# Output tiles in pairs: two-bank accumulators, one VectorE add and one store per pair, a fixed order, and all main stores on one queue

## The chip, the cores and the metric

The kernel runs on one core of one Trainium2 chip. The metric is the device time of one execution in microseconds. All runs quoted here are in the same (fast) state. Before the change the median is 433.73 us (433.66 to 433.82, four runs). A profile is a separate execution and its span is a little shorter than the timed one: 431.5 us for the kernel before.

## The reference

The first part is linear attention. The second part works on its result `x` (8 batches, 576 rows, 512 columns): a Fourier transform along the rows, a complex 512x512 weight for each of the lowest 64 modes, the inverse transform, and a channel product.

```python
def phi(v): return np.where(v > 0, v, np.exp(v) - 1.0) + 1.0
x = (phi(q) @ (phi(k).T @ v)) / (phi(q) @ phi(k).sum(rows) + 1e-6)      # per batch and head (shortened)
X = np.fft.rfft(x, axis=1)
Yr = np.einsum('bmd,mde->bme', Xr, w_r) - np.einsum('bmd,mde->bme', Xi, w_i)   # 64 modes
Yi = np.einsum('bmd,mde->bme', Xr, w_i) + np.einsum('bmd,mde->bme', Xi, w_r)
y = np.fft.irfft(Y, n=S, axis=1)
u = x + y
return u + np.maximum(u @ w_ch, 0.0)
```

## The kernel before

The two weights hold 134 MB in float32 and stream in through GpSimd's queue, with a cast on the way. For each mode four small matmuls per weight give the product. Almost everything else is worked off while the weights stream: `E` = x @ w_ch per output tile, the inverse transform of the modes that are done, and so on. When the last weight has landed, the last modes go into a small tile `last`, copies of its rows go by DMA into the tiles `YZ` of the batches, and the output stage begins.

The output stage has 36 tiles of 128x512: 32 main tiles, and four tail tiles made of the last 64 rows of two batches each. Per tile there is an identity matmul that adds `E` (L526), an inverse transform for the channel half (L507), a relu in place in the tile's accumulator in PSUM (ScalarE, L537; such an accumulator of 128x512 in float32 is called a bank here), a second inverse transform (L507), VectorE's add of `x` (L543), and a store (L548; a tail has two stores of half the partitions, L555). Main tiles are stored in twos, except the first two and the last two.

```python
def keep_warm(n):                                  # dummy matmuls; L333
    for _ in range(n):
        nc.tensor.matmul(last_ps[0], id16, wch16[:, 0, :])

def acc_bank(t):                                   # one bank per tile, from the pools of the weight stage
    ...
    return psW.tile([128, D], F32, tag=tag, bufs=bufs, name=f"acc{t}")

def begin(t, acc=None):
    if acc is None:
        acc = acc_bank(t)
        add_channels(acc, t)                       # E, identity matmul
        add_inverse(acc, t, 1)
    else:
        add_inverse(acc, t, 1, LATE)
    nc.scalar.activation(out=acc, in_=acc, func=AF.Relu)
    return acc

def end(t, acc, single):
    add_inverse(acc, t, 0)
    x = x_of(t)
    nc.vector.tensor_tensor(out=x, in0=acc, in1=x, op=ALU.add)
    ...                                            # main tiles: one store for two tiles unless single
        queue().dma_start(out=..., in_=x_main[b][:, j0 : jj + 1, :])
    ...                                            # tail tiles: two stores of 64 partitions
        (nc.sync, nc.gpsimd)[hf].dma_start(out=..., in_=x_tail[i][hf * 64 : hf * 64 + 64, :])

def queue():                                       # alternates
    return (nc.sync, nc.gpsimd)[n_queue % 2]

# in the mode loop, after mode NM - 5:
    last_ps += [bank("zl0"), bank("zl1")]          # buffers of the rotating tag "bank"
# in the last four modes keep_warm(6) is called after the first weight and after the product
```

A scheduler places the instructions of each engine by their dependencies. `pin` (short for `tc.keep_in_program_order`) fixes an instruction behind the pinned one traced before it on the same engine. The keep-warm matmuls and the output stage before the change are not pinned.

Of the kernel before, what the change touches and what calls it, by code (L numbers as in the profile page):

```python
# [10 lines left out]
F32 = mybir.dt.float32  # L11
F16 = mybir.dt.float16
BF16 = mybir.dt.bfloat16
AF = mybir.ActivationFunctionType
ALU = mybir.AluOpType
# [32 lines left out]
def kernel(  # L48
# [10 lines left out]
    nc = tc.nc  # L59

    B, H, S, Dh = q.shape
    D = H * Dh
# [3 lines left out]
    NJJ = 4  # L66
# [309 lines left out]
    psW = tc.alloc_tile_pool(name="psW", bufs=1, space=bass.MemoryType.PSUM)  # L376
# [23 lines left out]
    for kk in range(n_early):  # L400
# [6 lines left out]
        sW.tile([128, D], F32, tag="x_tail", bufs=B // 2, name=f"x_tail{i}") for i in range(B // 2)  # L407
# [4 lines left out]
    def x_of(t: int):  # L412
        return x_main[t // NJJ][:, t % NJJ, :] if t < B * NJJ else x_tail[t - B * NJJ]
# [10 lines left out]
    def bank(name: str, shape=(128, D), dtype=F32):  # L424
        return psW.tile(list(shape), dtype, tag="bank", bufs=5, name=name)
# [67 lines left out]
    n_acc = 0  # L493

    def acc_bank(t: int):
        nonlocal n_acc
        n = n_acc
        n_acc += 1
        tag, bufs = ("bank", 5) if n < N_PRE or (n - N_PRE) % 8 > 2 else (("P", 2), ("P", 2), ("yt", 1))[(n - N_PRE) % 8]
        return psW.tile([128, D], F32, tag=tag, bufs=bufs, name=f"acc{t}")  # L500

    N_PRE = 3
    EARLY, LATE, BOTH = 1, 2, 3

    def add_inverse(acc, t: int, half: int, what: int = BOTH):

        mm = lambda o, l, r: nc.tensor.matmul(  # L507
            o, l, r, start=False, stop=True, skip_group_check=True
        )
        if t < B * NJJ:  # L510
            parts = [(t // NJJ, slice(0, 128), slice(t % NJJ * 128, t % NJJ * 128 + 128))]
        else:
            i = t - B * NJJ
            parts = [(2 * i + h, slice(h * 64, h * 64 + 64), slice(512, 576)) for h in range(2)]
        for b, r, sel in parts:
            if b > 0:
                mm(acc[r, :], inv_sb[:, sel], YZ[b][:, half, :])
                continue
            if what & EARLY:
                mm(acc[r, :], inv_sb[: 2 * NE, sel], YZ[b][: 2 * NE, half, :])  # L520
            if what & LATE:
                mm(acc[r, :], inv0_sb[:, sel], last[:, half, :])

    def add_channels(acc, t: int):
        for cols, src in e0_parts(t):
            nc.tensor.matmul(  # L526
                acc[:, cols], id16, src, start=(cols.start == 0), stop=False, skip_group_check=True
            )

    def begin(t: int, acc=None):  # L530
        if acc is None:
            acc = acc_bank(t)
            add_channels(acc, t)
            add_inverse(acc, t, 1)
        else:
            add_inverse(acc, t, 1, LATE)
        nc.scalar.activation(out=acc, in_=acc, func=AF.Relu)  # L537
        return acc

    def end(t: int, acc, single: bool):  # L540
        add_inverse(acc, t, 0)
        x = x_of(t)
        nc.vector.tensor_tensor(out=x, in0=acc, in1=x, op=ALU.add)  # L543
        if t < B * NJJ:
            b, jj = divmod(t, NJJ)
            if jj % 2 == 1 or single:
                j0 = jj if single else jj - 1
                queue().dma_start(  # L548
                    out=out[b, 0:512, :].rearrange("(r j) d -> r j d", j=NJJ)[:, j0 : jj + 1, :],
                    in_=x_main[b][:, j0 : jj + 1, :],  # L550
                )
        else:
            i = t - B * NJJ
            for hf in range(2):
                (nc.sync, nc.gpsimd)[hf].dma_start(  # L555
                    out=out[2 * i + hf, 512:S, :], in_=x_tail[i][hf * 64 : hf * 64 + 64, :]
                )

    n_queue = 0

    def queue():
        nonlocal n_queue
        n_queue += 1
        return (nc.sync, nc.gpsimd)[n_queue % 2]

    order = []
    for i in range(B // 2):
        order += [2 * i * NJJ + jj for jj in range(2 * NJJ)]
        order.insert(len(order) - 2, B * NJJ + i)
    single = set(order[:2] + order[-2:])  # L570
    ready = {}
# [4 lines left out]
    for kk in range(n_early, NM):  # L576
# [9 lines left out]
        if kk == NM - 5:  # L586
            for t in order[:N_PRE]:
                acc = ready[t] = acc_bank(t)
                add_channels(acc, t)
                add_inverse(acc, t, 1, EARLY)  # L590
            last_ps += [bank("zl0"), bank("zl1")]


    y_ps = psW.tile([128, NDC, 128], F16, tag="P", bufs=2, name="ypl")
# [18 lines left out]
    for b in range(1, B):  # L613
        eng = nc.sync if b < 3 else nc.gpsimd
        eng.dma_start(out=YZ[b][2 * NE : 128, :, :], in_=last[b::B, :, :])  # L615


    SKEW = 2
    accs = {}
    for n in range(len(order) + SKEW):  # L620
        if n < len(order):
            accs[n] = begin(order[n], ready.get(order[n]))
        if n >= SKEW:
            t = order[n - SKEW]
            end(t, accs.pop(n - SKEW), t in single)
    psW.release()
# [29 lines left out]
```

## Time and profile before

| | before |
|---|---|
| time, median | 433.73 us |
| DMA share until 390 us | about 1.06 (full) |
| last weight landed | 394.0 us |
| first add of the output stage | 399.01 us |
| end of the last add | 424.6 us |
| span of the profile | 431.5 us |

The table by windows of the kernel before. Its columns are named in its first line; PEclk is the TensorE clock granted, 1.00 being full, and DMA share is how busy the 16 DMA engines were. In all views PE is TensorE and PEld its weight loads, DVE is VectorE, ACT ScalarE, POOL GpSimd and SP SyncE; L507 is line 507 of the kernel; a line of dots marks a cut.

```profile
core 0: us, PE busy (x) PEld busy (x) DVE busy (x) ACT busy (x) POOL busy (x), PEclk, DMA share, GB/s
340.00:344.00 4.00, 2.46 (x18) 1.06 (x15) 1.64 (x4) 0.72 (x2) 1.06 (x2) 0.50 1.06 213
...
384.00:388.00 4.00, 3.27 (x23) 1.34 (x23) 0.00 (x0) 0.58 (x1) 0.00 (x0) 1.00 1.07 214
...
396.00:400.00 4.00, 4.00 (x26) 2.02 (x24) 1.41 (x3) 3.01 (x6) 2.17 (x5) 1.00 0.14 40
400.00:404.00 4.00, 4.00 (x21) 1.45 (x20) 3.08 (x6) 2.82 (x5) 1.36 (x3) 1.00 0.64 238
404.00:408.00 4.00, 4.00 (x22) 1.77 (x19) 4.00 (x7) 3.37 (x6) 1.16 (x2) 1.00 0.86 311
408.00:412.00 4.00, 4.00 (x20) 1.61 (x19) 3.66 (x6) 3.15 (x7) 1.09 (x2) 1.00 0.97 386
...
428.00:432.00 4.00, 0.00 (x0) 0.00 (x0) 0.00 (x0) 0.00 (x0) 0.00 (x0) 0.50 0.06 21
```

At 340 us and at 384 us the DMA engines are full (share 1.06 and 1.07): the weights bound the kernel there, and the matmuls have time to spare (TensorE is busy for 2.46 and 3.27 us of the 4). Note the clock: 0.50 at 340 us, 1.00 at 384 us. From 396 us the output stage runs; TensorE is busy for the whole of each window, and the DMA engines fill up with stores (311 GB/s, then 386).

The dummy matmuls are one group in the view by lines; its last part says when they ran.

```profile
L333 PE MATMUL zl_3714<-wch_67,id_64 x42: 376/379/390, 378.4 to 393.1; 128*128 128x512 f16 x42
```

They stand between 378 and 393 us, in the gaps in which TensorE waits for weights, and the clock is full there (1.00 in every window from 376 to 394 us).

The chain of waits of the kernel before, from the last weight towards the output stage (start, length, what ran; `zl` is the last modes' channel product):

```profile
394.05 0.39 PE P_0_3815 L348 x4
...
395.65 0.61 PE zl_3714 L601 x4
396.26 0.44 PE zl_3715 L601 x4
```

The timeline of VectorE, of ScalarE, and of TensorE in the kernel before (start, length, engine, line, operation):

```profile
399.01 0.69 DVE L543 TENSOR_TENSOR x_main_1602<-acc_3705,x_main_1602 128x512 f32<-128x512 f32 x1 [1.86 <-PE acc_3705 L507]
399.62 0.68 DVE L543 TENSOR_TENSOR x_main_1602<-acc_3708,x_main_1602 128x512 f32<-128x512 f32 x1
...
397.71 0.58 ACT L537 ACTIVATE acc_3705<-acc_3705 128x512 f32<-128x512 f32 x1 [0.18 <-PE acc_3705 L507]
398.21 0.58 ACT L537 ACTIVATE acc_3708<-acc_3708 128x512 f32<-128x512 f32 x1
...
405.18 0.38 PE L507 MATMUL acc_3942<-YZ_1616,inv_sb 128*128 128x512 f16 x1
405.40 0.38 PE L507 MATMUL acc_3929<-YZ_1616,inv_sb 128*128 128x512 f16 x1
```

Back-to-back adds start 0.61 us apart and back-to-back relus 0.50. A matmul of 512 columns starts every 0.215 us at full clock, so the three of a main tile take 0.645 us: TensorE sets the pace of production, by a little. In the view of TensorE's waits there is no entry for the kernel before between 398 and 424 us; around a tail a few matmuls start 0.31 to 0.34 us apart instead of 0.215. The stores need 9.44 MB at up to 400 GB/s (401 from 415 to 416 us), 23.6 us by that rate: nearly as long as the 25.6 us from the first add to the end of the last.

### The profile page before, as it was taken

How to read it: one execution, taken by the hardware profiler on the slowest of the kernel's cores; microseconds unless marked ns; L12 is line 12 of the kernel's file. 1: busy time of each engine (PE TensorE's matmuls, PEld its weight loads, DVE VectorE, ACT ScalarE, POOL GpSimd, SP SyncE). 2: the span in 40 equal slices, each digit the busy share in tenths (PEclk: the TensorE clock that was granted, in tenths of full speed). 3: DMA queues.
4: the chain of work that ended last, by engine and by line, in shares of the span. 5: the costliest groups of instructions: out<-in, count | busy, mean ns of one | idle time of the engine just before them, and what ended most of it. 6: DMA issues, size and time to landing. Idle time of an engine off the chain costs nothing. (4 is left out here: it accounts for less than half of the span.)

```text
span 431.5 us, 6261 instructions
## 1 busy us (share of the span) xinstructions
PE 296.4 (69%) x2544; PEld 153.4 (36%) x2544; DVE 178.7 (41%) x350; ACT 148.8 (34%) x228; POOL 97.8 (23%) x176
## 2 busy tenths in 40 slices
PE   0359677796028677667776767657588759987992
PEld 0347556573004233222322223223233227833340
DVE  1699998954004232322322223223223212202893
ACT  3687666621003222222223222122222221302781
POOL 4232322122112212211222112112112120201321
PEclk9999766666559766685658577586855566999998
DMA  9999999999999999999999999999999999993796
GB/s 151 208 208 209 209 209 209 212 213 218 218 212 213 214 214 213 213 214 214 213 213 213 214 215 213 214 213 213 213 213 213 214 214 213 213 213 70 283 347 263
DMA packets 35468, 92.36 MB, mean 214 GB/s; under 512 B 3200, under 2 KB 16384, under 8 KB 35440
## 3 DMA queue, kind: packets, MB, share of 16 engines
q0 software_dynamic: 33184, 86.69, 100.5%
q1 hardware_dynamic: 2256, 5.28, 3.6%
q8 instruction: 20, 0.33, 0.3%
q14 instruction: 8, 0.07, 0.0%
HBM read 164.07 MB, written 9.44 MB: 402 GB/s over the span
## 5 line engine op out<-in xcount | busy, mean ns | idle before, releaser
L348 PEld LDWEIGHTS <-xt_c 128*32 128x32 bf16 x520 | 25.0, 164 | 64.8 <-issue 27.6
L362 PE MATMUL yt_1445<-pick_sb,ys_1446 128*128 128x16 f16 x4 | 0.3, 174 | 21.0 <-DMA pick_sb<-row_pick 21.0
L507 PEld LDWEIGHTS <-inv_sb 128*128 128x128 f16 (+3 forms) x90 | 7.8, 99 | 11.2 <-issue 4.5
L333 PE MATMUL zl_3714<-wch_67,id_64 128*128 128x512 f16 x42 | 10.6, 380 | 0.0
L358 DVE CAST ys_1476<-P_0_1477 128x512 f16<-128x512 f32 x1 | 0.7, 691 | 23.5 <-PE P_0_1477 L348 23.5
L211 PE MATMUL qTp_0_147<-id_64,qe_122 128*128 128x128 f16 x9 | 1.1, 311 | 11.5 <-DVE qe_122 L195 11.5
L360 ACT CAST ys_1491<-P_0_1492 128x512 f16<-128x512 f32 x1 | 0.6, 585 | 23.7 <-PE P_0_1492 L348 23.7
L480 PEld LDWEIGHTS <-YT 128*112 128x112 f16 x32 | 7.8, 291 | 1.8 <-issue 1.4
L362 PEld LDWEIGHTS <-ys_1446 128*128 128x128 f16 x4 | 0.3, 104 | 21.0 <-issue 20.9
L484 PEld LDWEIGHTS <-YT 128*112 128x112 f16 x32 | 7.5, 294 | 0.5
L146 PEld LDWEIGHTS <-qT_102 64*128 64x128 f16 (+1 forms) x80 | 2.8, 129 | 10.2 <-ACT qT_102 L218 4.7
L211 PEld LDWEIGHTS <-qe_122 128*128 128x128 f16 x18 | 1.8, 146 | 11.5 <-DVE qe_122 L195 11.5
L146 PEld LDWEIGHTS <-qT_105 64*128 64x128 f16 (+1 forms) x80 | 3.0, 129 | 7.9 <-issue 6.5
L526 PEld LDWEIGHTS <-id_64 128*128 128x128 f16 x40 | 3.9, 98 | 4.8 <-issue 1.2
L615 POOL DMA_DIRECT2D YZ_1617<-last x1 | 0.5, 509 | 20.2 <-ACT last L612 20.2
L146 PEld LDWEIGHTS <-qT_106 64*128 64x128 f16 (+1 forms) x80 | 2.6, 125 | 6.8 <-issue 4.8
L146 PEld LDWEIGHTS <-qT_108 64*128 64x128 f16 (+1 forms) x80 | 2.5, 124 | 6.7 <-issue 5.2
L333 PEld LDWEIGHTS <-id_64 128*128 128x128 f16 x42 | 3.3, 97 | 4.1 <-issue 1.4
L146 PE MATMUL num_0_223<-kv_75,qT_102 64*128 64x65 f16 x8 | 0.6, 233 | 5.9 <-ACT kv_75 L242 5.9
L146 PEld LDWEIGHTS <-qT_107 64*128 64x128 f16 (+1 forms) x80 | 2.4, 120 | 6.2 <-issue 4.6
L146 PEld LDWEIGHTS <-qT_103 64*128 64x128 f16 (+1 forms) x80 | 2.9, 128 | 4.4 <-issue 3.8
L146 PEld LDWEIGHTS <-qT_104 64*128 64x128 f16 (+1 forms) x80 | 2.4, 121 | 5.4 <-issue 4.2
(1406 smaller groups left out, 880.8 us busy)
## 6 DMA issues: line engine op xcount, KB each, us to landing
q_0_110<-in_q_dram POOLq DMA_DIRECT2D x1, 576.0 KB, 6.4
k_0_112<-in_k_dram POOLq DMA_DIRECT2D x1, 576.0 KB, 8.4
v_0_114<-in_v_dram POOLq DMA_DIRECT2D x1, 576.0 KB, 10.4
q_1_116<-in_q_dram POOLq DMA_DIRECT2D x1, 576.0 KB, 12.5
k_1_118<-in_k_dram POOLq DMA_DIRECT2D x1, 576.0 KB, 14.6
v_1_120<-in_v_dram POOLq DMA_DIRECT2D x1, 576.0 KB, 16.8
q_2_141<-in_q_dram POOLq DMA_DIRECT2D x1, 576.0 KB, 12.1
k_2_143<-in_k_dram POOLq DMA_DIRECT2D x1, 576.0 KB, 12.0
```

The costliest lines, as they stand in the source:

```text
L146: mm = nc.tensor.matmul(num[hpo][orow, c0 : c0 + 65], qT[rows, hpp, h2, cols], kv_sb[rows, hpp, h2, :])
L211: nc.tensor.transpose(qT_ps[:, j].rearrange("p t r -> p (t r)"), phi["q", b][:, hpp, j].rearrange("p o d -> p (o d)"), id16,)
L333: nc.tensor.matmul(last_ps[0], id16, wch16[:, 0, :])
L348: nc.tensor.matmul(P[i][dc * 32 : dc * 32 + 32, :], xt_cols(dc, t, kk), w[:, dc, i * pw : i * pw + pw], start=(t == 1), stop=(t == 0), til ...
L358: nc.vector.tensor_copy(out=dst, in_=P[i])
L360: nc.scalar.copy(out=dst, in_=P[i])
L362: nc.tensor.matmul(yt_ps[:, ec, kk % 8, :], st[:, ec * 128 : ec * 128 + 128], pick_sb)
L480: nc.tensor.matmul(z_ps[: 2 * NE, :], lhs[ec], wch16[:, ec, :], start=(ec == 0), stop=(ec == NDC - 1))
L484: nc.tensor.transpose(y_ps[: 2 * NE, ec, :], lhs[ec], id16)
L507: mm = lambda o, l, r: nc.tensor.matmul(o, l, r, start=False, stop=True, skip_group_check=True)
L526: nc.tensor.matmul(acc[:, cols], id16, src, start=(cols.start == 0), stop=False, skip_group_check=True)
L615: eng.dma_start(out=YZ[b][2 * NE : 128, :, :], in_=last[b::B, :, :])
```

## The change

Its intent is to take the output stage in pairs of tiles. A pair shares a two-bank accumulator, so VectorE can add 1024 columns in one instruction and there is one store per pair. All matmuls, relus and adds of the stage are pinned in a fixed order. All main stores go out on SyncE's queue. Tail tiles are paired too, so each half of the partitions stores two batches at once. Batch 0's last rows are now copied by DMA like the others', which spares its later tiles a second matmul per half. The PSUM pools are split so that the accumulators get pools of their own; `zl0` gets a bank of its own by the way.

The core of the diff, cut and in places condensed:

```diff
-    return psW.tile(list(shape), dtype, tag="bank", bufs=5, name=name)
+    return psB.tile(list(shape), dtype, tag="bank", bufs=4, name=name)
...
+pairs = []                       # main pairs; a pair of tails before the last pair of batches 3 and 7
+def channels(n):
+    pool = acc_pools[n % 4 // 2]
+    accs[n] = pool.tile([128, 2, D], F32, tag="acc", bufs=2, name=f"acc{n}")
+    ...                          # E of both tiles, pinned
+def rectified(n):
+    for i, t in enumerate(pairs[n]):
+        add_inverse(accs[n][:, i], t, 1, LATE if n < N_PRE else BOTH)     # pinned
+    for i in range(2):
+        a = accs[n][:, i]
+        pin(nc.scalar.activation(out=a, in_=a, func=AF.Relu))
+def store(t, n_t):
+    ...
+        nc.sync.dma_start(out=..., in_=x_main[b][:, jj : jj + n_t, :])
+    ...
+    for hf in range(2):
+        (nc.sync, nc.gpsimd)[hf].dma_start(
+            out=out[2 * i + hf : 2 * i + 4 : 2, 512:S, :].rearrange("b r d -> r b d"),
+            in_=x_tail[i // 2][hf * 64 : hf * 64 + 64, :, :])
+def finish(n):
+    single = n in (0, len(pairs) - 1)
+    for i, t in enumerate(pairs[n]):
+        add_inverse(acc[:, i], t, 0)     # with EARLY and LATE for the first two pairs
+        if single:
+            pin(nc.vector.tensor_tensor(out=x_of(t), in0=acc[:, i], in1=x_of(t), op=ALU.add)); store(t, 1)
+    if not single:
+        pin(nc.vector.tensor_tensor(out=x, in0=acc, in1=x, op=ALU.add)); store(t0, 2)   # 1024 columns
...
-            last_ps += [bank("zl0"), bank("zl1")]
+            last_ps.append(psW.tile([128, D], F32, tag="zl", bufs=1, name="zl0"))
...
-    for b in range(1, B):
+    for b in (1, 2, 3, 4, 5, 6, 7, 0):                # copies of last into YZ
...
+    for n in range(4, len(pairs)):
+        channels(n); rectified(n); finish(n - 1)
```

More of the change, by code (lines that the diff above doesn't have):

```diff
@@ L375 @@
     sA_ctx.close()
-    psW = tc.alloc_tile_pool(name="psW", bufs=1, space=bass.MemoryType.PSUM)
+    PSUM = bass.MemoryType.PSUM
+    psW = tc.alloc_tile_pool(name="psW", bufs=1, space=PSUM, side="left")
+    psB = tc.alloc_tile_pool(name="psB", bufs=1, space=PSUM, side="right")
     n_early = n_keep + n_pre
@@ L406 @@
     x_tail = [
-        sW.tile([128, D], F32, tag="x_tail", bufs=B // 2, name=f"x_tail{i}") for i in range(B // 2)
+        sW.tile([128, 2, D], F32, tag="x_tail", bufs=B // 4, name=f"x_tail{i}") for i in range(B // 4)
     ]
@@ L412, in x_of @@
     def x_of(t: int):
-        return x_main[t // NJJ][:, t % NJJ, :] if t < B * NJJ else x_tail[t - B * NJJ]
+        if t < B * NJJ:
+            return x_main[t // NJJ][:, t % NJJ, :]
+        i = t - B * NJJ
+        return x_tail[i // 2][:, i % 2, :]
     def e0_parts(t: int):
@@ L492 @@
     last = sW.tile([128, 2, D], F16, tag="last", bufs=1, name="last")
-    n_acc = 0
-    def acc_bank(t: int):
-        nonlocal n_acc
-        n = n_acc
-        n_acc += 1
-        tag, bufs = ("bank", 5) if n < N_PRE or (n - N_PRE) % 8 > 2 else (("P", 2), ("P", 2), ("yt", 1))[(n - N_PRE) % 8]
-        return psW.tile([128, D], F32, tag=tag, bufs=bufs, name=f"acc{t}")
-    N_PRE = 3
     EARLY, LATE, BOTH = 1, 2, 3
     def add_inverse(acc, t: int, half: int, what: int = BOTH):
-        mm = lambda o, l, r: nc.tensor.matmul(
-            o, l, r, start=False, stop=True, skip_group_check=True
+        mm = lambda o, l, r: pin(
+            nc.tensor.matmul(o, l, r, start=False, stop=True, skip_group_check=True)
         )
@@ L515, in add_inverse @@
         for b, r, sel in parts:
-            if b > 0:
+            if what == BOTH:
                 mm(acc[r, :], inv_sb[:, sel], YZ[b][:, half, :])
@@ L522, in add_inverse @@
                 mm(acc[r, :], inv0_sb[:, sel], last[:, half, :])
-    def add_channels(acc, t: int):
-        for cols, src in e0_parts(t):
-            nc.tensor.matmul(
-                acc[:, cols], id16, src, start=(cols.start == 0), stop=False, skip_group_check=True
-            )
-    def begin(t: int, acc=None):
-        if acc is None:
-            acc = acc_bank(t)
-            add_channels(acc, t)
-            add_inverse(acc, t, 1)
-        else:
-            add_inverse(acc, t, 1, LATE)
-        nc.scalar.activation(out=acc, in_=acc, func=AF.Relu)
-        return acc
@@ L540, in end, with channels @@
-    def end(t: int, acc, single: bool):
-        add_inverse(acc, t, 0)
-        x = x_of(t)
-        nc.vector.tensor_tensor(out=x, in0=acc, in1=x, op=ALU.add)
+    pairs = []
+    for b in range(B):
+        pairs += [(b * NJJ, b * NJJ + 1), (b * NJJ + 2, b * NJJ + 3)]
+        if b % 4 == 3:
+            k = b // 4
+            pairs.insert(len(pairs) - 1, (B * NJJ + 2 * k, B * NJJ + 2 * k + 1))
+    N_PRE = 2
+    acc_pools: list = []
+    accs: dict[int, object] = {}
+    def channels(n: int):
+        pool = acc_pools[n % 4 // 2]
+        accs[n] = pool.tile([128, 2, D], F32, tag="acc", bufs=2, name=f"acc{n}")
+        for i, t in enumerate(pairs[n]):
+            for cols, src in e0_parts(t):
+                pin(
+                    nc.tensor.matmul(
+                        accs[n][:, i, cols], id16, src, start=(cols.start == 0), stop=False,
+                        skip_group_check=True,
+                    )
+                )
@@ L544, in end, with rectified, store @@
+    def rectified(n: int):
+        for i, t in enumerate(pairs[n]):
[3 more added lines that the diff above has]
+            pin(nc.scalar.activation(out=a, in_=a, func=AF.Relu))
+    def store(t: int, n_t: int):
         if t < B * NJJ:
             b, jj = divmod(t, NJJ)
-            if jj % 2 == 1 or single:
-                j0 = jj if single else jj - 1
-                queue().dma_start(
-                    out=out[b, 0:512, :].rearrange("(r j) d -> r j d", j=NJJ)[:, j0 : jj + 1, :],
-                    in_=x_main[b][:, j0 : jj + 1, :],
-                )
-        else:
-            i = t - B * NJJ
-            for hf in range(2):
-                (nc.sync, nc.gpsimd)[hf].dma_start(
-                    out=out[2 * i + hf, 512:S, :], in_=x_tail[i][hf * 64 : hf * 64 + 64, :]
-                )
@@ L559 @@
-    n_queue = 0
-    def queue():
-        nonlocal n_queue
-        n_queue += 1
-        return (nc.sync, nc.gpsimd)[n_queue % 2]
-    order = []
-    for i in range(B // 2):
-        order += [2 * i * NJJ + jj for jj in range(2 * NJJ)]
-        order.insert(len(order) - 2, B * NJJ + i)
-    single = set(order[:2] + order[-2:])
-    ready = {}
+            nc.sync.dma_start(
+                out=out[b, 0:512, :].rearrange("(r j) d -> r j d", j=NJJ)[:, jj : jj + n_t, :],
+                in_=x_main[b][:, jj : jj + n_t, :],
+            )
@@ new lines, in store, with finish @@
+            return
+        i = t - B * NJJ
+        for hf in range(2):
+            (nc.sync, nc.gpsimd)[hf].dma_start(
+                out=out[2 * i + hf : 2 * i + 4 : 2, 512:S, :].rearrange("b r d -> r b d"),
+                in_=x_tail[i // 2][hf * 64 : hf * 64 + 64, :, :],
+            )
+    def finish(n: int):
+        acc = accs.pop(n)
+        single = n in (0, len(pairs) - 1)
+        t0 = pairs[n][0]
+        for i, t in enumerate(pairs[n]):
+            if n < N_PRE:
+                add_inverse(acc[:, i], t, 0, EARLY)
+                add_inverse(acc[:, i], t, 0, LATE)
+            else:
+                add_inverse(acc[:, i], t, 0)
+            if single:
+                x = x_of(t)
+                pin(nc.vector.tensor_tensor(out=x, in0=acc[:, i], in1=x, op=ALU.add))
+                store(t, 1)
+        if single:
+            return
+        x = x_main[t0 // NJJ][:, t0 % NJJ : t0 % NJJ + 2, :] if t0 < B * NJJ else x_tail[(t0 - B * NJJ) // 2]
+        pin(nc.vector.tensor_tensor(out=x, in0=acc, in1=x, op=ALU.add))
+        store(t0, 2)
@@ L586 @@
         if kk == NM - 5:
-            for t in order[:N_PRE]:
-                acc = ready[t] = acc_bank(t)
-                add_channels(acc, t)
-                add_inverse(acc, t, 1, EARLY)
-            last_ps += [bank("zl0"), bank("zl1")]
+            psB.release()
+            acc_pools.append(
+                tc.alloc_tile_pool(name="psT0", bufs=1, space=PSUM, side="right", reuse_waits="tile")
+            )
+            for n in range(N_PRE):
+                channels(n)
+                for i, t in enumerate(pairs[n]):
+                    add_inverse(accs[n][:, i], t, 1, EARLY)
+            last_ps.append(psW.tile([128, D], F32, tag="zl", bufs=1, name="zl0"))
+    last_ps.append(psW.tile([128, D], F32, tag="P", bufs=2, name="zl1"))
     y_ps = psW.tile([128, NDC, 128], F16, tag="P", bufs=2, name="ypl")
@@ L612 @@
     pin(nc.scalar.copy(out=last[:, 0, :], in_=y_ps.rearrange("p c r -> p (c r)")))
-    for b in range(1, B):
-        eng = nc.sync if b < 3 else nc.gpsimd
+    for b in (1, 2, 3, 4, 5, 6, 7, 0):
+        eng = nc.sync if b in (1, 2) else nc.gpsimd
         eng.dma_start(out=YZ[b][2 * NE : 128, :, :], in_=last[b::B, :, :])
-    SKEW = 2
-    accs = {}
-    for n in range(len(order) + SKEW):
-        if n < len(order):
-            accs[n] = begin(order[n], ready.get(order[n]))
-        if n >= SKEW:
-            t = order[n - SKEW]
-            end(t, accs.pop(n - SKEW), t in single)
-    psW.release()
+    psW.release()
+    acc_pools.append(
+        tc.alloc_tile_pool(name="psT1", bufs=1, space=PSUM, side="left", reuse_waits="tile")
+    )
+    rectified(0)
+    rectified(1)
+    channels(2)
+    finish(0)
+    channels(3)
+    finish(1)
+    rectified(2)
+    rectified(3)
+    finish(2)
+    for n in range(4, len(pairs)):
+        channels(n)
+        rectified(n)
+        finish(n - 1)
+    finish(len(pairs) - 1)
+    acc_pools[1].release()
+    acc_pools[0].release()
 _INS = ['q', 'k', 'v', 'moe_w_r', 'moe_w_i', 'moe_w_ch']
```

## The prediction

> **What bounds the kernel now.** The table by windows shows the 16 DMA engines full (1.06) until 390 us of the 431.5 us span. The last weight load lands at 394.0 us and the chain of waits starts from it: 3.5 us of short steps to `last` (397.5), then the output stage. There the timeline shows TensorE issuing one 512-column matmul every 0.215 us without a gap: three per tile, 0.645 us per main tile, 6.28 us per nine tiles. VectorE's add (0.69 us, 0.61 when back to back) and ScalarE's relu (0.58) fit under that. The stores are a second limit of nearly the same size: 9.44 MB, and from 408 us the DMA share is 0.9 to 1.0 at up to 400 GB/s, so 23.6 us at best; store landing times grow from 2.7 to about 6 us. Last add issued 423.9, last packets about 428 to 429, span end 431.5.
>
> **What the change does.** The casts give VectorE a slope of about 1.05 ns per column (128x256 0.42, 128x512 0.69), so a pair's add should take about 1.23 us against 1.30 for two: about 1 to 2 us less VectorE work over the stage, off the critical path because TensorE needs 1.29 us per pair. Loading batch 0's last rows by DMA removes extra matmuls for the later tiles of batch 0, and fixed order with pairs fills the small TensorE bubbles around tails: worth about 1 us of TensorE time. Stores on one queue: intervals in which only SyncE's packets ran already reach 400 GB/s, so no loss expected[...].
>
> **What it also does, unintended.** The instruction order shows that the 42 keep-warm matmuls (unpinned, target `zl`, which now has a bank of its own without earlier users) are hoisted from the last four modes to the early modes. They filled the load waits from 376 to 394 us, where the granted clock is 1.00. Without them TensorE has some 1.3 us of work per 4.8 us there. Around 340 to 352 us, with TensorE 61 to 73% busy, the clock is 0.50. So I expect 0.50 from about 385 [...] ([...] the trace's clock has only 0.5 and 1.0). Cost: `last` about 1.2 us later, then about 1 us more in the first matmuls at 0.43 us each: 2 to 2.5 us in all for the first stores.
>
> **Sum.** Production starts 2 to 2.5 us later, then runs about 1.29 us per pair; stores take about 1.31 us per pair. Before, the DMA engines were underfed for about 2 us between 401 and 408, and this slack and the smoother tails absorb most of the delay. I expect last packets at about 429: 434.6 us, range 432.3 to 437.0. The weight stage stays DMA bound with four banks rather than five.
>
> **Signs.** Granted clock 0.50 in 386 to 398 [...]; keep-warm matmuls absent after 376, present before 250; `last` at about 398.7; pair add 1.2 us; first add about 401.5 (399.0 before); DMA share near 1.0 to the end; load stage end unchanged at 394.
>
> **What would make it wrong.** A single store queue not filling the DMA engines (slower by far more); the hoisted matmuls or four banks delaying weight loads; the clock staying warm (then about 432); tail stores of 64 partitions colliding differently.
>
> Chances: faster by over 2% 0.01, within 2% 0.96, slower by over 2% 0.03.

That the clock would stay at half through the first matmuls of the output stage, from which the cost of 2 to 2.5 us follows, was the author's estimate; that a matmul of 512 columns starts every 0.43 us at half clock is in the trace of the kernel before (L457, four in 1.89 us from 343.3 us). The sum: it came to 434.6 us, 0.9 above the kernel before.

## The result, and the profile after

The change makes the kernel slower: 437.32 us (436.75 to 437.66, four runs) against 433.73. The ratio is 1.0078, with a 95% interval of 1.0064 to 1.0093. Ratios here are the mean time of one kernel's fast runs over that of the other's in the same rounds, so they are not quite the ratio of the medians. The prediction was 434.6 us and at most 437.0: the difference it foretold (+0.9 us) is a quarter of the measured one (+3.6 by the medians, +3.4 by the ratio).

The same table by windows for the kernel after, with the same columns.

```profile
384.00:388.00 4.00, 1.62 (x12) 0.56 (x12) 0.00 (x0) 0.59 (x1) 0.00 (x0) 0.50 1.07 214
...
396.00:400.00 4.00, 3.82 (x17) 2.03 (x16) 0.42 (x1) 1.65 (x4) 1.04 (x3) 0.50 0.02 5
400.00:404.00 4.00, 3.15 (x15) 1.28 (x14) 1.48 (x3) 1.54 (x3) 1.86 (x4) 1.00 0.38 127
404.00:408.00 4.00, 3.15 (x16) 1.33 (x15) 2.85 (x3) 3.13 (x6) 0.00 (x0) 1.00 0.50 197
...
428.00:432.00 4.00, 0.07 (x1) 0.00 (x0) 0.69 (x1) 0.00 (x0) 0.00 (x0) 0.84 0.92 286
432.00:436.00 4.00, 0.00 (x0) 0.00 (x0) 0.00 (x0) 0.00 (x0) 0.00 (x0) 0.50 0.10 39
```

Three things differ. At 384 us the clock is 0.50, and it stays there until 400 us. From 400 to 408 us TensorE is busy for 3.15 us of each 4, although its clock is full again; before it was busy throughout. And the stores of these eight microseconds run at 127 and 197 GB/s, against 238 and 311. The DMA engines then have work until 432 us; before they had finished soon after 428.

The dummy matmuls after the change:

```profile
L333 PE MATMUL zl<-wch,id x42: 376/379/634, 129.8 to 166.3; 128*128 128x512 f16 x42
```

They ran 227 to 249 us too early. Their bank `zl` no longer has earlier users to wait for, and nothing pins them, so the scheduler is free to put them early; the pinned variants below hold them back.

The chain of waits after the change:

```profile
393.90 0.71 PE P L348 x7
...
395.73 1.90 PE zl L616 x8
...
398.23 1.87 PE acc L503 x4
...
401.22 0.70 DVE x_main L575
401.97 0.59 PE acc L503 x2
```

The eight matmuls into `zl` take 1.90 us instead of 0.61 + 0.44, and the first four matmuls of the output stage take 1.87 us: they start 0.43 us apart, twice the 0.215 us of full clock. The first add comes at 401.22 us, 2.2 us later than before. The profiled execution is the fastest of the four (436.75 us), and the moment at which the clock rises is not the same in every cold execution: 400.0 us here, about 401.5 in b_nowarm below (worked out from its 0.81 over 400 to 404 us).

The timeline after the change, of the same three engines:

```profile
401.22 0.69 DVE L575 TENSOR_TENSOR x_main<-acc,x_main 128x512 f32<-128x512 f32 x1 [3.14 <-PE acc L503]
402.60 0.69 DVE L575 TENSOR_TENSOR x_main<-acc,x_main 128x512 f32<-128x512 f32 x1 [0.68 <-PE acc L503]
403.90 1.22 DVE L580 TENSOR_TENSOR x_main<-acc,x_main 128x1024 f32<-128x1024 f32 x1 [0.61 <-PE acc L503]
...
404.33 2.30 ACT L546 ACTIVATE acc<-acc 128x512 f32<-128x512 f32 x4 [2.76 <-PE acc L503]
...
401.97 0.38 PE L503 MATMUL acc<-YZ,inv_sb 112*128 112x512 f16 x1 [0.85 <-DVE x_main L575]
405.58 0.59 PE L503 MATMUL acc<-YZ,inv_sb 128*128 128x512 f16 x2 [0.85 <-ACT acc L546]
```

The bracket at the end of a line is the idle time of the engine before it and what ended it. The pair's add takes 1.22 us, as predicted. But the second add comes 1.38 us after the first, where before it came after 0.61. TensorE's first matmul of the second tile, at 401.97, waited for the add of the *first* tile of the pair, whose bank it does not touch. The one at 405.58 waited for a pair's relus. The view of TensorE's waits between 400 and 429 us, empty before, now has two lines (total, times, longest):

```profile
PE acc L503 <- DVE x_main L575: 1.7, 2, 0.9
PE acc L503 <- ACT acc L546: 1.6, 2, 0.9
```

Apart from these waits, groups of two pair adds start at 406.21 and 408.94 us, so a pair takes 1.37 us, against 1.29 for two tiles before. From the first add to the end of the last are 27.6 us, against 25.6 before.

Lastly the stores. The windows around a tail of the kernel before (its stores are issued at 417.1 and 417.4 us), and then around the first pair of tails after the change (issued at 414.5 and 414.8 us):

```profile
415.00:416.00 1.00, 1.00 (x7) 0.34 (x5) 1.00 (x2) 0.77 (x3) 0.53 (x1) 1.00 1.01 401
...
418.00:419.00 1.00, 1.00 (x6) 0.46 (x5) 1.00 (x2) 0.87 (x3) 0.28 (x1) 1.00 1.04 397
419.00:420.00 1.00, 1.00 (x6) 0.48 (x5) 1.00 (x3) 0.94 (x2) 0.31 (x1) 1.00 0.96 238
```

```profile
415.00:416.00 1.00, 1.00 (x5) 0.38 (x4) 0.81 (x1) 0.90 (x2) 0.42 (x1) 1.00 0.27 86
416.00:417.00 1.00, 1.00 (x6) 0.48 (x5) 0.97 (x1) 0.72 (x3) 0.00 (x0) 1.00 1.00 201
417.00:418.00 1.00, 1.00 (x6) 0.40 (x5) 0.93 (x2) 0.97 (x2) 0.00 (x0) 1.00 1.07 279
418.00:419.00 1.00, 1.00 (x6) 0.39 (x5) 0.78 (x2) 0.87 (x3) 0.00 (x0) 1.00 0.93 299
```

Slow tails are not new: in the kernel before, too, the engines count as full at 419 us and yet move 238 GB/s. After the change there is first a gap in the supply of stores (share 0.27), and then three such microseconds in a row, 259 GB/s on average, against 397 and more from 419 us on. And the view of the stores shows SyncE's issues (shortest, median, longest in ns):

```profile
L551 SPq DMA_DIRECT2D out_dram<-x_main x18: 332/332/2074, 401.9 to 428.8; - x18
```

One issue took 2.07 us instead of 0.33; it is the last main store, which follows the second pair of tails.

### The profile page after: what moved, and what is told of

Read it like the earlier page. It is cut to its first block, busy times and chain, and to the rows that moved or that the text cites. A ratio compares the mean times of both kernels' runs of the same rounds, so it can differ in the third digit from the quotient of the medians.

```text
span 435.0 us, 6218 instructions
## 1 busy us (share of the span) xinstructions
PE 291.6 (67%) x2542; PEld 153.5 (35%) x2542; DVE 177.2 (41%) x334; ACT 149.4 (34%) x228; POOL 92.5 (21%) x166
## 4 chain that ended last, share of the span: by engine, by line
DMA 67%; PE 16%; DVE 8%; issue 5%; ACT 2%; POOL 1%; POOLq 0%; DVEq 0%; ACTq 0%
DMA wr<-in_moe_w_r_dram 34%; DMA wi<-in_moe_w_i_dram 25%; DMA k<-in_k_dram 7%; PE acc L503 4%; PE P L348 3%; DVE x L265 3%; PE eps L462 2%; PE z L485 2%; PE acc L535 2%; PE yp L489 1%; DVE qe L195 1%; DVE q L189 1%; DVE k L189 1%; DVE rd L262 1%; DVE ke L195 1%
## 5 line engine op out<-in xcount | busy, mean ns | idle before, releaser
L114 POOL DMA_DIRECT2D wr<-in_moe_w_r_dram x64 | 34.1, 533 | 136.0 <-PE P L348 112.5
L348 PE MATMUL P<-wi,xt_c 128*32 128x512 bf16 (+1 forms) x260 | 40.7, 525 | 32.0 <-DMA wi<-in_moe_w_i_dram 31.9
L348 PE MATMUL P<-wr,xt_c 128*32 128x512 bf16 (+1 forms) x260 | 42.4, 539 | 27.0 <-DMA wr<-in_moe_w_r_dram 25.7
L470 ACT CAST E<-eps 128x512 f16<-128x512 f32 (+1 forms) x40 | 21.4, 544 | 113.8 <-PE eps L462 113.8
L462 PE MATMUL eps<-wch,xTw 128*128 128x512 f16 x144 | 57.7, 545 | 2.5 <-DVE xTw L459 2.3
L114 POOL DMA_DIRECT2D wi<-in_moe_w_i_dram x64 | 34.1, 534 | 102.9 <-PE P L348 73.9
L447 DVE TENSOR_TENSOR x_main<-nw,rd 128x256 f32<-128x256 f32 x64 | 24.2, 420 | 67.2 <-PE nw L146 67.1
L348 PEld LDWEIGHTS <-xt_c 128*32 128x32 bf16 x520 | 25.8, 161 | 71.7 <-issue 42.4
L358 DVE CAST ys<-P 128x512 f16<-128x512 f32 (+1 forms) x33 | 22.5, 682 | 67.3 <-PE P L348 67.2
L546 ACT ACTIVATE acc<-acc 128x512 f32<-128x512 f32 x36 | 20.8, 582 | 6.9 <-PE acc L503 6.0
L265 DVE TENSOR_TENSOR x<-num,rd 128x512 f16<-128x512 f32 x32 | 22.1, 692 | 1.1
```

The lines of the kernel that those rows point to most:

```text
L114: nc.gpsimd.dma_start(out=w, in_=src[kk].rearrange("(p dc) e -> p dc e", dc=NDC))
L265: nc.vector.tensor_tensor(out=dst.rearrange("p (o c d) -> p o c d", o=2, c=4), in0=nv[:, :, :, 0:64], in1=rden.unsqueeze(3).broadcast_to([ ...
L348: nc.tensor.matmul(P[i][dc * 32 : dc * 32 + 32, :], xt_cols(dc, t, kk), w[:, dc, i * pw : i * pw + pw], start=(t == 1), stop=(t == 0), til ...
L358: nc.vector.tensor_copy(out=dst, in_=P[i])
L447: nc.vector.tensor_tensor(out=x[orow, o * 256 : o * 256 + 256].rearrange("p (c d) -> p c d", c=4), in0=nv[o][:, :, 0:64], in1=rd_all[b][or ...
L462: nc.tensor.matmul(e_ps, xT[:, c, :], wch16[:, c, :], start=(c == 0), stop=(c == NDC - 1))
```

## The experiments

My theory after the result had four parts that could each cost something, and each is a rival of the others for the 3.4 us: (A) the cold clock that delays the start, (B) waits for the whole two-bank accumulator, (C) the single store queue, (D) the tail stores. The rival of A was the prediction's own view, that a delay of the start is absorbed later, because DMA was underfed for a while anyway. Times below are medians; each ratio is to the kernel before in the same rounds. The runs were made on three chips, so compare ratios, not medians, across runs. A ratio step of 0.001 is 0.43 us. The intervals are about 0.6 us wide to each side, so a difference of two ratios is uncertain by some 0.9 us. Edits are cut to their core.

### A: the start

**b_nowarm**, the kernel before without the dummy matmuls:

```diff
-        for _ in range(n):
+        for _ in range(0):
```

> The kernel before with the keep-warm matmuls taken out and nothing else. Theory 1: clock 0.50 from about 384 until about 400, first add about 401 instead of 399.0, and most of that delay reaches the end: 435.3 to 436.0. Rival A (the store stage hides it, as I had predicted: part of the delay is absorbed by DMA slack before 408): 433.7 to 434.5.

Measured: 435.92 us, ratio 1.0047 (1.0033 to 1.0061), so +2.0 us. VectorE's first adds and the windows of this run:

```profile
401.86 2.65 DVE L543 TENSOR_TENSOR x_main<-acc,x_main 128x512 f32<-128x512 f32 x4 [3.67 <-PE acc L507]
...
400.00:404.00 4.00, 4.00 (x18) 1.65 (x17) 2.07 (x4) 2.08 (x6) 2.08 (x5) 0.81 0.22 62
404.00:408.00 4.00, 4.00 (x20) 1.45 (x21) 3.23 (x6) 3.12 (x7) 0.94 (x2) 1.00 0.87 342
```

The clock is cold as in the kernel after (0.50 from 383 to 386 us; it is full only in the course of the first window shown). The store traffic of 404 to 408 us here has the same share (0.87) as that of the same window before (0.86), but the windows ahead of it are emptier (0.22 at 400 us against 0.64). So the slow filling of the DMA engines belongs to the start of production and for the most part moves with it. The first add came 2.85 us later than before (401.86 against 399.01) and the last one ended 2.8 us later (427.35 against 424.58); of this, 2.0 us reached the time. By these single profiles some 0.8 us at most was absorbed, which is about the noise. The rival, that most of the delay is absorbed, falls.

**a_warm**, the change with the dummy matmuls pinned:

```diff
-            nc.tensor.matmul(last_ps[0], id16, wch16[:, 0, :])
+            tc.keep_in_program_order(nc.tensor.matmul(last_ps[0], id16, wch16[:, 0, :]))
```

> The changed kernel with one edit: the keep-warm matmuls are kept behind the mode matmuls that precede them in the program, so they stand in the last four modes again. Theory 1 (the cold clock is one of three causes): granted clock 1.00 from about 360 to the end of TensorE's work, first add at about 399.0 instead of 401.2, everything after it about 2.2 us earlier, time about 435.0. Rival A (the store queue alone decides the end): clock and first add change the same way but the time stays at 437 +- 0.4. Rival B (the clock is all of it): time about 433 or less.

Measured: 439.51 us, ratio 1.0135 (1.0117 to 1.0154). It became slower, but the experiment was flawed. TensorE's timeline:

```profile
389.65 5.28 PE L333 MATMUL zl<-wch,id 128*128 128x512 f16 x12
...
396.25 0.47 PE L348 MATMUL P<-wr,xt_c 128*32 128x256 bf16 x8
```

Twelve dummies stood in one block of 5.28 us at half clock, and held up the product of the last mode's first weight until 396.25 us. The run measured its own delay and says nothing about the clock. The pins of only one kind of instruction had fixed them relative to each other, not to the mode matmuls around them.

**a_warm2**, the same with the matmuls of the last four modes pinned too, and the dummies spread between them:

```diff
-            nc.tensor.matmul(last_ps[0], id16, wch16[:, 0, :])
+            pin(nc.tensor.matmul(last_ps[0], id16, wch16[:, 0, :]))
...
+        late = pin if kk >= NM - 4 else (lambda i: i)     # around the two matmul groups of a mode
...
+        if NM - 4 <= kk < NM - 1:
+            keep_warm(4)                                  # ahead of the pick matmuls
...
-            keep_warm(6)
+            keep_warm(2)                                  # behind them
```

> The changed kernel with the keep-warm matmuls between the mode matmuls of the last four modes exactly as before the change (6 after the first weight, 4 after the second, 2 after the picks); the earlier attempt put 12 of them in a row ahead of the last mode and so delayed it. Theory 1: clock 1.00 throughout from about 364, first add about 399.0, and as removing keep-warm cost the kernel before 2.0 us, time about 2 us below the change: 435.0 to 435.7. Rival A (clock hidden in the changed kernel): 437.0 to 437.6.

Measured: 435.40 us, ratio 1.0035 (1.0021 to 1.0049). That is 0.0043 below the change, about 1.9 us. Between 383 and 386 us the clock is 1.00 again. The first add comes at 399.78 us and the last one ends at 427.36, both 1.44 us earlier than in the change, and here nothing of it is lost on the way to the time. A is worth about 2 us, from both sides: taking the dummies away from the kernel before costs it, putting them back into the change returns it. In the change the clock was at half for 17 us, from 383 to 400, and that costs only these 2 us or so of 433.7, since most of the matmul time at the end of the weight stage was spare (from 386 to 390 us TensorE was busy for 1.34 us of 4 even at half clock). It showed where nothing was spare: the first add came 2.2 us later, although the last weight had landed at 394 us as before.

### B: the two-bank accumulators

**a_singles**, in which the first and last pair run all four inverse matmuls ahead of their two adds:

```diff
-            if single:
+        if single:
+            for i, t in enumerate(pairs[n]):
                 x = x_of(t)
...
-        if single:
             return
```

> The changed kernel, in the first and last pair both tiles' last matmuls are issued before the two adds, so TensorE no longer waits 0.85 and 0.88 us for VectorE to read the other half of the same two-bank accumulator. Theory 1: the two waits vanish, second add about 0.9 us earlier at the start, last add about 0.5 to 1.4 us earlier, time 436.2 to 436.8. Rival A (queue alone): 437.2 +- 0.3, because the last stores stand behind the tail stores in the queue anyway.

Measured: 436.30 us, ratio 1.0064 (1.0050 to 1.0078). The waits for VectorE's add are gone, and from the first add to the end of the last are 25.8 us. But in this profile the clock rose only at about 402 us and the first add came at 403.01, so the last one ended at 428.77 us, where it ended in the change (428.80). The time moved by 0.6 us, which the intervals do not separate from the change.

**a_relu**, one relu of 1024 columns per pair:

```diff
-        for i in range(2):
-            a = accs[n][:, i]
-            pin(nc.scalar.activation(out=a, in_=a, func=AF.Relu))
+        a = accs[n]
+        pin(nc.scalar.activation(out=a, in_=a, func=AF.Relu))
```

> The changed kernel with one relu over both banks of a pair instead of two. Relu of a pair about 1.05 us instead of 1.20; TensorE's wait of about 0.2 us in every other pair vanishes and the steady step falls from 1.37 to about 1.29 us per pair. Theory 1 (TensorE waiting for the whole accumulator costs about 1 us over the stage): last add about 1 us earlier, time 436.2 to 436.7. Rival A (store queue and DMA decide): adds end earlier but time 437.2 +- 0.3.

Measured: 436.94 us, ratio 1.0077 (1.0065 to 1.0090): no gain. The step did fall to 1.29 us per pair, as expected, but the four waits stayed (3.2 us in all).

**a_onebank** keeps the pairs, the order and the stores, but gives each tile a one-bank accumulator and an add of its own:

```diff
-        accs[n] = pool.tile([128, 2, D], F32, tag="acc", bufs=2, name=f"acc{n}")
+        accs[n] = [pool.tile([128, D], F32, tag="acc", bufs=4, name=f"acc{n}_{i}") for i in range(2)]
...
+            pin(nc.vector.tensor_tensor(out=x, in0=acc[i], in1=x, op=ALU.add))     # for each tile
...
-        pin(nc.vector.tensor_tensor(out=x, in0=acc, in1=x, op=ALU.add))
         store(t0, 2)
```

> The changed kernel with a one-bank accumulator per tile in place of the two-bank one, and so one add per tile; order, clock, pools, store sizes and queue as in the change. Theory 1 (an accumulator of two banks makes every engine wait for both halves): no TensorE wait for VectorE in first and last pair, steady step about 1.29 us per pair instead of 1.37, first to last add about 25 us instead of 27.6, time 434.5 to 435.8. Rival A (the pairing of adds is harmless or a gain, clock and tails are the loss): 437 or more, because VectorE gets 1 to 2 us more work.

Measured: 435.48 us, ratio 1.0038 (1.0022 to 1.0053), 0.0040 below the change: 1.7 us. The view of TensorE's waits is empty for this run between 400 and 429 us. Its timeline:

```profile
398.76 2.05 ACT L546 ACTIVATE acc<-acc 128x512 f32<-128x512 f32 x4 [0.18 <-PE acc L503]
...
401.63 2.59 DVE L574 TENSOR_TENSOR x_main<-acc,x_main 128x512 f32<-128x512 f32 x4 [3.64 <-PE acc L503]
```

Four relus take 2.05 us where they took 2.30, the adds follow each other again, and first add to the end of the last is 24.8 us (401.63 to 426.41) instead of 27.6. The first add is 0.4 us later than in the change's profile, so the last one ends 2.4 us earlier, and of these 1.7 reached the time: the profile's span ends 7.3 us behind the last add here, and 6.2 us behind it after the change, so the stores have begun to hold it up. So B is real. The edit takes away the shared tile and the shared add together, so it does not price them one by one; the waits that it removes are those of the two lines above.

### C: the store queue

**a_twoq**, the change with main stores alternating between SyncE's and GpSimd's queue, and **b_oneq**, the kernel before with all of them on SyncE's:

```diff
-            nc.sync.dma_start(
+            (nc.sync, nc.gpsimd)[stored[0] % 2].dma_start(          # a_twoq; stored[0] counts the stores
```

```diff
-        return (nc.sync, nc.gpsimd)[n_queue % 2]
+        return nc.sync                                              # b_oneq
```

> The changed kernel with the main stores alternating between the queues of SyncE and GpSimd, as before the change. Theory 1: the store issues that took 0.75, 1.02, 0.82 and 2.07 us behind a tail store fall to below 0.6 us, last packets about 0.5 to 1.5 us earlier, time 435.8 to 436.8. Rival A (the single queue is the whole loss): 433.5 to 434.5. Rival B (clock only): 437.3 +- 0.3.

> The kernel before with all main stores on SyncE's queue, tails as they were (one half on each queue). Theory 1 (one queue costs little by itself, about half a us through store issues held up behind tail stores): 433.7 to 434.8. Rival A (the single queue is the loss): 436 or more.

Measured: a_twoq 437.96 us, ratio 1.0097 (1.0081 to 1.0114), not clearly different from the change; b_oneq 432.41 us, ratio 0.9963 (0.9948 to 0.9977), a gain of 1.6 us. One queue is no cost; in the kernel before it is a gain, which I had not expected, and a_twoq, 0.8 us slower than the change, points the same way. In b_oneq's view of the stores and its windows:

```profile
L548 SPq DMA_DIRECT2D out_dram<-x_main x18: 332/332/512, 399.5 to 424.3; - x18
...
DMA to landing us min/median/max: 2.4/2.9/4.4
```

```profile
400.00:404.00 4.00, 4.00 (x21) 1.41 (x20) 3.08 (x6) 2.82 (x5) 0.00 (x0) 1.00 0.75 279
```

The first store goes out at 399.5 us. In the kernel before, the first two went out at 400.24 (GpSimd, behind its copies of `last`, as the chain of waits shows) and 400.33. Its stores took 3.5 us to land in the median and 6.4 at most, against 2.9 and 4.4 here, and moved 238 GB/s in this window against 279. How much of the gain is the earlier start and how much the quicker landing was not separated. In b_oneq_again (below) the first store went out at 400.0 us, only 0.2 us earlier than in the kernel before, and the landing times were again 2.9 and 4.5 us, which speaks for the landing.

### D: the tail stores

**a_tailpool** puts both tail stores on GpSimd's queue, so that no main store stands behind one of them in SyncE's:

```diff
-            (nc.sync, nc.gpsimd)[hf].dma_start(
+            nc.gpsimd.dma_start(
```

> The changed kernel with both halves of each tail store on GpSimd's queue, so SyncE's queue holds main stores only. If the 2 KB tail packets in SyncE's queue are what holds up the stores behind them: SyncE's issues are 0.33 us throughout, last packets about 1 us earlier, time 436.0 to 436.6. If the loss is the half-partition source and not the queue: low DMA rate around each tail store as before, time 437.2 +- 0.4.

Measured: 437.50 us, ratio 1.0082 (1.0067 to 1.0098): no gain. SyncE's longest issue fell from 2.07 to 0.80 us, but the DMA engines still moved only 184 and 176 GB/s from 416 to 418 us. Getting the main stores out from behind the tail's in SyncE's queue does not help by itself.

**a_tailsplit** stores each tail pair by four stores of one batch instead of two of two batches:

```diff
-        for hf in range(2):
-            (nc.sync, nc.gpsimd)[hf].dma_start(
-                out=out[2 * i + hf : 2 * i + 4 : 2, 512:S, :].rearrange("b r d -> r b d"),
-                in_=x_tail[i // 2][hf * 64 : hf * 64 + 64, :, :],
-            )
+        for j in range(2):
+            for hf in range(2):
+                (nc.sync, nc.gpsimd)[hf].dma_start(
+                    out=out[2 * (i + j) + hf, 512:S, :],
+                    in_=x_tail[i // 2][hf * 64 : hf * 64 + 64, j, :],
+                )
```

> The changed kernel with each tail pair stored by four stores of 128 KB (one per batch, as before the change) instead of two of 256 KB. If the paired access pattern is what makes tail stores slow: DMA rate around them as before the change, about 1 us gained, 436.0 to 436.6. If 64 partitions as the source are the cause: no change, 437.3 +- 0.4.

Measured: 436.34 us, ratio 1.0059 (1.0045 to 1.0074), 0.8 us below the change; the two intervals overlap a little. The windows of this run for the same tails:

```profile
416.00:417.00 1.00, 1.00 (x6) 0.47 (x5) 1.00 (x1) 0.75 (x2) 0.00 (x0) 1.00 0.99 305
417.00:418.00 1.00, 1.00 (x6) 0.39 (x4) 0.93 (x2) 0.97 (x2) 0.00 (x0) 1.00 0.94 272
418.00:419.00 1.00, 1.00 (x6) 0.45 (x5) 0.78 (x2) 0.87 (x3) 0.00 (x0) 1.00 1.01 401
```

The three microseconds move 326 GB/s on average instead of 259, and no main store's issue takes longer than 0.65 us. At the second pair, which ends the kernel, there is no such gain (262 GB/s from 428 to 432 us, against 286). Bytes and partitions are the same, so at the first pair the shape of the store matters; which part of it (its size, its two-batch access, how the halves mix) stays open. That D costs time is not shown by this run alone; a_best below repeats it.

### Together

**a_comb** joins a_warm's edit, a_singles, a_relu and a_twoq.

> The changed kernel with four of the edits together: keep-warm held in place, both tiles' matmuls ahead of the adds in first and last pair, one relu per pair, main stores alternating between two queues. Theory 1: the parts add up, about -2.2 -0.7 -0.8 -0.7 us: 432.5 to 433.5, at or a little below the kernel before. Rival A (one cause is the whole loss, and the rest hides behind it): no better than the best single edit by more than 0.5 us.

Measured: 437.91 us, ratio 1.0083 (1.0063 to 1.0103), with the first add at 403.77 us. It contains a_warm's flaw and proves nothing about the sum.

**a_warm2_onebank** joins a_warm2 and a_onebank, and **a_best** adds a_tailsplit.

> The two edits of a_warm2 and a_onebank together. Theory 1: their gains add, 432.2 to 433.6, that is below the kernel before and about as fast as the kernel before with all main stores on one queue. Rival A (something else of the change still costs over 1 us): 434.5 or more.

> The changed kernel with keep-warm as before, one-bank accumulators and tail pairs stored by four stores: all three repairs, all main stores still on one queue. If the three causes are the whole loss and add up (-1.9, -1.8, -0.9 us from 437.3): 432.4 to 433.0, level with the kernel before with one queue. If a further loss hides in the change: 433.3 or more.

Measured: 433.32 us, ratio 0.9990 (0.9976 to 1.0003), and 432.12 us, ratio 0.9969 (0.9957 to 0.9981). The parts add up: 0.0088 for A and B together against 0.0043 + 0.0040 one by one. And the split tail stores gain 0.9 us here (0.9990 to 0.9969) after 0.8 alone. Again the first tails are faster (324 GB/s over three microseconds against 244) and the last are not. SyncE's longest issue is 1.36 us in a_best. A repetition, **a_best_again**, gave 432.29 us, ratio 0.9960 (0.9946 to 0.9974).

> a_best once more on the same chip as a_best_tail4b: 431.9 to 432.6, ratio to the kernel before 0.996 to 0.998.

So a_best is faster than both kernels, by 1.3 to 1.7 us than the one before. The next two runs ask where that comes from. **a_best_twoq** is a_best with a_twoq's edit; **b_oneq_again** repeats b_oneq.

> As a_best, with the main stores alternating between the queues of SyncE and GpSimd. If one queue is a true gain of the change, as in the kernel before (-1.5 us): 0.8 to 1.8 us slower than a_best. If the queue does not matter in the changed order, as the twin run on the change suggested: equal within 0.5 us.

> The kernel before with all main stores on SyncE's queue once more, on the same chip as the three others: 432.0 to 432.8 by the first run of it.

Measured: 433.59 us, ratio 1.0009 (0.9996 to 1.0021), and 432.50 us, ratio 0.9979 (0.9966 to 0.9992). With two queues a_best is just the kernel before; with one queue the kernel before comes within 0.4 us of a_best. Within the noise all of a_best's advantage is the one queue, and the one line of b_oneq gets it. One queue also fills the DMA engines: a_best moves 397 GB/s from 416 to 420 us, where SyncE issues main stores only.

Last, whether pairing the tails costs anything beyond the shape of their stores. **a_best_tail4** takes four single tails, in the places of the kernel before, and **a_best_tail4b** also moves the copy for batch 0 forward:

```diff
-        if b % 4 == 3:
-            k = b // 4
-            pairs.insert(len(pairs) - 1, (B * NJJ + 2 * k, B * NJJ + 2 * k + 1))
+        if b % 2 == 1:
+            pairs.insert(len(pairs) - 1, (B * NJJ + b // 2,))       # both
...
-    for b in (1, 2, 3, 4, 5, 6, 7, 0):
+    for b in (1, 2, 0, 3, 4, 5, 6, 7):                               # a_best_tail4b only
```

> As a_best, but the four tail tiles stand singly at the places they had before the change, each stored by two stores of 128 KB. If it is the grouping of tails into two bursts of 512 KB that fills the queue ahead of the last stores: 431.5 to 432.4, a little below a_best. If not: equal to a_best within 0.4 us.

> As a_best_tail4, with batch 0's last rows copied first on GpSimd's queue instead of last. In a_best_tail4 TensorE waited 2.2 us for that copy at the first tail and the clock fell to 0.50 from 405.4 to 408.9. If that wait was the whole of its loss: no such wait, clock 1.00 to the end of the work, time equal to a_best or up to 0.6 us below it (431.5 to 432.4). If single tails cost by themselves: 433 or more.

Measured: 435.98 us, ratio 1.0052 (1.0036 to 1.0067). The first tail waited 2.2 us for the copy of batch 0's rows, which comes last, and the clock fell to half once more from 405.4 to 408.9 us, so this run was another flawed one. With the copy moved: 432.76 us, ratio 0.9971 (0.9958 to 0.9983), equal to a_best within the intervals. Pairing the tails is harmless in itself.

## Why the prediction was wrong

**What it had right.** The dummy matmuls are hoisted (it expected them before 250 us; they ran from 130 to 166). The granted clock is 0.50 from 383 us (it said about 385) to 400. The first add comes at 401.22 us (it said 401.5), the last weight lands at 394, a pair's add takes 1.22 us (1.23), and the saving on VectorE lies off the critical path. Over windows that hold no switch the clock is only ever 0.50 or 1.00, and TensorE was busy nearly without a gap from 395.7 us, 4.3 us before the clock rose at 400.0. What it takes for the clock to rise was not shown.

**The step that failed** is this one: "this slack and the smoother tails absorb most of the delay". The slack of about 2 us between 401 and 408 us was read as a reserve. It is the filling of the store pipeline after the first add, and in b_nowarm it moved along with the first add, for the most part. Most of the delay was passed on and not absorbed: +2.0 us for adds that came 2.8 us late in b_nowarm, -1.9 us for adds that came 1.4 us earlier in a_warm2. And the tails were not smoother but a cost, as below.

**A term with the wrong sign** is "fixed order with pairs fills the small TensorE bubbles around tails", with production at 1.29 us per pair. Before, the view of TensorE's waits had no entry in this stage, and the bubbles around a tail were about 0.1 us each, so there was little to fill. The pairs brought four waits of up to 0.9 us, 3.3 us in all, and a step of 1.37 us per pair, and first add to last add grew by 2.0 us. The cause shown by the trace and removed by a_onebank is that a wait is kept for the tile, and the tile is now two banks: a matmul into one bank waits for an add or a relu of the other. Giving each tile its own bank and its own add returned 1.7 us. In a_onebank the waits are by bank, TensorE has none between 400 and 429 us, and the result is correct: the wait was wider than needed.

**A risk named but not costed**: "tail stores of 64 partitions colliding differently". Their new shape cost about 0.8 us by a_tailsplit and 0.9 by a_best against a_warm2_onebank; each is near the noise, and they agree. The change's tail stores, each of half the partitions, are slow (259 GB/s over three full microseconds, against 397 and more for main stores from 419 us on), but the kernel before had the same halves, and a_tailsplit, with them too, moves 326, so the halves alone are not the explanation.

**A neutral term that is a gain**: "Stores on one queue: ... no loss expected". It is true that there is no loss. The four comparisons give 1.6, 0.9, 1.7 and 0.8 us in favour of one queue (b_oneq, its repetition, a_best against a_best_twoq, and the change against a_twoq, the last not clear of noise).

The sum: +2.0 (clock) +1.7 (tile-wide waits) +0.8 (tail stores) -1.3 (one queue, the mean of the four) is +3.2 us, against +3.4 by the ratio. With 0.6 to 0.9 us of uncertainty on each part this agreement is partly luck. Better evidence that no large cause is missing is that a_best, the change with A, B and D repaired, is level with the kernel before on one queue, within 0.4 us. The change was slow because of what came along with it: the pair add, its core, saves VectorE time that nobody waited for.

## What to carry to other kernels

When a buffer is given a bank of its own, look at what its old neighbours held in place: here the unpinned matmuls, left without a wait, went to the front (from 378 us to 130), and the warm-up warmed nothing there (clock 0.50 from 383 to 400 us). Slack behind the start of a bound stage is no reserve for a late start, unless it stays where it is when the start moves (in b_nowarm it moved along, and 2.0 of 2.8 us were passed on); one run that delays only the start tells. And before merging two buffers to merge two instructions, ask which engine is the limit: here the merge saved time on the engine that shares the instruction (1.22 us for a pair's add, against 1.29 from the start of one single add to the end of the next), and cost overlap on those that share the buffer (four waits of TensorE, 3.3 us in all).
